# Expert-outer tile order, weights two deep, sorts inside the first expert, and PSUM banks evicted in pairs, in a fused Fourier-mixing and expert kernel

## The chip, the cores and the metric

The kernel runs on one core of a Trainium2 chip. The metric is the time of one execution on the device in microseconds (us); lower is better. An execution varies by about 1% (the unchanged kernel on chip A: 655.30 to 660.46). The runs of this study fell on at least four chips, called A to E here (A's number is not on record, so A may be D or E), and the unchanged kernel doesn't take the same time on all of them: 657.55 us on A, 696.86 on B, 695.48 on C, 659.18 on D, 658.26 on E (medians). So times are compared only with runs of the unchanged kernel in the same rounds on the same chip, and between chips only landmarks inside the traces are compared.

Engines are named as in the profile: PE is TensorE, PEld its weight loads, DVE VectorE, ACT ScalarE, POOL GpSimd, SP SyncE. PSUM is the memory that TensorE writes its results to; a *bank* is a tile of 512 f32 values for each of 128 partitions here. A result is *evicted* when ScalarE or VectorE copies it out, after which its bank is written again (in the first sorts after the change TensorE waits 0.90 to 2.13 us at a time for that). The *granted clock* is the profile's figure for the share of TensorE's full speed that was granted to it (0.50 to 0.98 in the stretches shown before the experiments). A weight is *turned* when TensorE multiplies it by a fixed matrix before its first use.

## The reference, cut to what matters

```python
def _attn_ref(x):                          # x: (8, 2496, 256)
    X = np.fft.fft(np.fft.fft(x, axis=1), axis=2)
    return X.real
def _moe_ref(x, w_gate, w1, w2):           # x: (19968, 256); 8 experts, F = 1024
    cap = N // E
    order = np.argsort(-(x @ w_gate).flatten())
    for idx in order:                      # best score first
        tok, e = idx // E, idx % E
        if assigned[tok] >= 0 or counts[e] >= cap: continue
        assigned[tok] = e; counts[e] += 1
    for e in range(E):
        out[assigned == e] = np.maximum(x[assigned == e] @ w1[e], 0.0) @ w2[e]
```

The kernel does the transform as matrix products. Tokens whose expert the first selection settles are sorted by expert with 0/1 matrices (five "strips" of sorted tokens) and form 40 *early tiles* of up to 384 tokens. The others are settled by further selection rounds, mostly VectorE work, which run while TensorE does early tiles. When the rounds are over, the tokens' places are computed (an "inverse placement"), and 16 *late tiles* are gathered from DRAM by GpSimd. Every 128 output rows go out through one indirect scatter, also issued by GpSimd: 168 scatters and 48 gathers in all.

## The kernel before

A PSUM bank is its own tile here:

```python
    def big_ps(nm):
        return spread_ps("h", 3, [P, 512], FT, nm)      # 3 banks, one more later on
    def transform(n):
        ps = []
        for r in range(2):                              # two halves, two banks
            fps = big_ps("fftps").rearrange("p (b d) -> p b d", b=NB)
            ...                                         # 20 matmuls into fps
            ps.append(fps)
        nc.scalar.copy(ev, ps[0])
        nc.vector.tensor_tensor(st[:, :, 0, :], ev, ps[1], op=AL.add)
        nc.vector.tensor_tensor(st[:, :, 3, :], ev, ps[1], op=AL.subtract)
    def up(d, fcs):                                     # first expert matmul, tile "hps"
        for fc in fcs:
            hps = big_ps("hps")
            ...                                         # 2 matmuls
            take(d["hid"][:, fc, 0:n], hps[:, 0:n], True)   # eviction on ScalarE or VectorE
```

`take` gives an eviction to whichever of ScalarE and VectorE has less to do by an estimate kept while the program is built. `down` makes the second expert matmul (tile `ops`), evicts it to an output buffer `ot` (8 of them), and scatters that. A tile is worked off in three parts ("thirds"); the order of tiles is strip by strip, and the gathers come in threes from tile 28 on:

```python
            for part, (fcs, b0) in enumerate((((0, 1, 2), 0), ((3, 4, 5), P), ((6, 7), 2 * P))):
                for step in aside.get((j, part), ()):
                    step()                              # sorts, weights, gathers
                up(tiles[j], fcs)
                down(tiles[j - 1], b0, group)
                pace()                                  # some of the selection rounds
    tiles = [early_tile(t, e) for t in range(NT) for e in range(E)]
    G0 = 28
    for m, d in enumerate(late):
        j = G0 + (3 * m) // 2 if m < 8 else 40 + m - 8
        at(j, 1, lambda d=d: (place_all(), gather(d)))
```

Of the kernel before, what the change touches and what calls it, by code (L numbers as in the profile page):

```python
# [18 lines left out]
B = 8  # L19
# [34 lines left out]
KC = 64  # L54
SYNC = None
# [11 lines left out]
def kernel(  # L67
# [14 lines left out]
    MAN = {mybir.EngineType.PE, mybir.EngineType.DVE, mybir.EngineType.Activation, mybir.EngineType.Pool}  # L82

# [174 lines left out]
    for b in range(B):  # L258
# [29 lines left out]
        if b % 4 == 3:  # L288
            for n0, nn in ((0, 4), (4, 4), (8, 2)):
                ytp = psl.tile([P, 4, P], FT, tag="tp", bufs=4, name="ytp")  # L290
                for u in range(nn):
                    nc.tensor.transpose(ytp[:, u, :], yt[:, n0 + u, :], identf)
                src = ytp[:, 0:nn, :].rearrange("p n (b f) -> p n b f", f=32)
                for s_ in range(2):
                    dh = yhl[:, n0:n0 + nn, s_, 0, :].rearrange("p n (b e) -> p n b e", e=E)[:, :, b - 3:b + 1, :]
                    dl = yhl[:, n0:n0 + nn, s_, 1, :].rearrange("p n (b e) -> p n b e", e=E)[:, :, b - 3:b + 1, :]
                    sv = src[:, :, :, s_ * E:(s_ + 1) * E]
                    nc.scalar.copy(dh, sv)
                    nc.vector.tensor_tensor(dl, sv, dh, op=AL.subtract)
        for i, r in tab_plan[b + 1]:  # L300
# [6 lines left out]
    lg = asg_c.tile([P, E, GC], FT, name="lg")  # L307
    with tc.tile_pool(name="pslog", bufs=1, space=PS) as pslog:
# [43 lines left out]
    def misc():  # L352
        return psr[0].tile([P, 512], FT, tag="misc", bufs=1, name="misc")
# [7 lines left out]
    def big_ps(nm):  # L361
        return spread_ps("h", 3, [P, 512], FT, nm)
# [21 lines left out]
    mv = asg.tile([P, GC], FT, name="mv")  # L384
    mvv = mv.rearrange("p (b q k) -> p b q k", b=B, q=4)
    nc.gpsimd.memset(mv, -1.0e9)  # L386
    tail0 = asg.tile([P, 1], FT, name="tail0")
    tail1 = asg.tile([P, 1], FT, name="tail1")
    head1 = asg.tile([P, 1], FT, name="head1")
    nc.gpsimd.tensor_scalar(tail0, in0=iota_p, scalar1=113.0, scalar2=2.0e9, op0=AL.is_ge, op1=AL.mult)  # L390
    nc.gpsimd.tensor_scalar(tail1, in0=iota_p, scalar1=112.0, scalar2=2.0e9, op0=AL.is_ge, op1=AL.mult)
    nc.gpsimd.tensor_scalar(head1, in0=is0, scalar1=2.0e9, scalar2=None, op0=AL.mult)
    for q in range(4):
        nc.gpsimd.tensor_scalar(mvv[:, :, q, NK - 1], in0=mvv[:, :, q, NK - 1],
                                scalar1=tail0 if q < 2 else tail1, scalar2=None, op0=AL.add)
        if q % 2 == 1:
            nc.gpsimd.tensor_scalar(mvv[:, :, q, 0], in0=mvv[:, :, q, 0], scalar1=head1, scalar2=None, op0=AL.add)


# [19 lines left out]
    rampw_i = asg.tile([P, EW + 2], I32, name="rampw_i")  # L419
# [5 lines left out]

    def payloads():
        pay_i = rampw_i[:, 0:GC]
        nc.gpsimd.iota(rampw_i, pattern=[[1, EW + 2]], base=1, channel_multiplier=0)
        nc.gpsimd.tensor_copy(rampw, rampw_i)
        for q, (s1, s2) in enumerate(((0, 1), (2, -1), (1, -1), (1, 1))):  # L430
            for par in range(2):
                nc.gpsimd.iota(pay_i.rearrange("p (n k b q) -> p n k b q", n=4, k=NK, b=2)[:, :, :, par, q],
                               pattern=[[2 * S, 4], [s2 * P, NK]], base=PAY0 + S // 2 * s1 + par * S,
                               channel_multiplier=s2)
        nc.vector.tensor_scalar(pay_i, in0=pay_i, scalar1=16, scalar2=None, op0=AL.logical_shift_left)
        nc.vector.tensor_copy(payr, pay_i.bitcast(FT))
        for n in range(4):
            nc.gpsimd.iota(pay_i[:, n * 8 * NK:(n + 1) * 8 * NK].rearrange("p (f k) -> p f k", k=NK),
                           pattern=[[1, 8], [8, NK]], base=n * 8 * NK + 1, channel_multiplier=0)
        nc.vector.tensor_copy(place, pay_i)  # L440
        for n in range(4):
            nc.gpsimd.iota(pay_i[:, n * 8 * NK:(n + 1) * 8 * NK].rearrange("p (f k) -> p f k", k=NK),
                           pattern=[[1, 8], [8 * P, NK]], base=n * 8 * P * NK + PAY0, channel_multiplier=8)
        nc.vector.tensor_scalar(pay_i, in0=pay_i, scalar1=16, scalar2=None, op0=AL.logical_shift_left)
        nc.vector.tensor_copy(payb, pay_i.bitcast(FT))
# [16 lines left out]
    def choose(first):  # L462
# [19 lines left out]
        yield SYNC  # L482
        for e in range(E):
            nc.scalar.activation(cjunk, dd[:, e, :], ACT.Relu, bias=1.0, scale=K_CNT, accum_out=cnt[:, e:e + 1])  # L484
            busy["A"] += 0.33
            if e % 4 == 3:
                yield 0.3
        nc.scalar.copy(cnt_x.rearrange("p (e g) -> p e g", g=NG), cnt[:, :, None].to_broadcast([P, E, NG]))
        yield SYNC
# [3 lines left out]
        chosen["src"] = src  # L493
# [3 lines left out]
    def lowest():  # L497
        nc.vector.scalar_tensor_tensor(wa, in0=dd, scalar=K_LOW, in1=chosen["src"], op0=AL.mult, op1=AL.subtract)
        yield 1.4
        for e in range(E):  # L500
            nc.vector.max(lists[:, e, :], wa[:, e, :])
            nc.scalar.copy(lists_x[:, :, e * NG:(e + 1) * NG], lists[:, e, :, None].to_broadcast([P, 8, NG]))
            busy["A"] += 0.3
            if e % 4 == 3:
                yield 1.0
        yield SYNC
        lt = psr[0].tile([P, 8, P], FT, tag="lt", bufs=1, name="lt")
# [4 lines left out]
        yield SYNC  # L512
# [64 lines left out]
    def raise_first(aside):  # L577
        run(lowest())
        run(search(2))
        aside(found["low"], found["wid"], found["lo0"])  # L580

        def finish():
            yield from search(1)
            yield from settle()
        return finish
# [46 lines left out]
    def inverse(hi1, lo1, pay, w, ncol):  # L632
        ramp8 = ramps[8]
        inv_ps = psr[0].tile([P, 512], FT, tag="lt", bufs=1, name="inv_ps")
        for c0 in range(0, ncol, 8):
            cs = slice(c0, c0 + 8)
            oh = moe.tile([P, 2, P * 8], BF, tag="w1raw", bufs=2, name="oh")
            o_lo = oh[:, 0, :].rearrange("p (a b) -> p a b", b=8)
# [68 lines left out]
    def first_strips(low, wid, lo0):  # L707
# [8 lines left out]
        nc.vector.scalar_tensor_tensor(lev, in0=lev, scalar=moved, in1=fits, op0=AL.min, op1=AL.max)  # L716
        bps = psm.tile([P, 512], FT, tag="o", bufs=1, name="lev_ps")
# [6 lines left out]
                                       op0=AL.is_ge, op1=AL.mult)  # L724
        v = asg.tile([P, GC], FT, tag="sl_v", bufs=1, name="sl_v")
# [22 lines left out]
        nc.vector.scalar_tensor_tensor(spot, in0=v, scalar=1.0, in1=has, op0=AL.add, op1=AL.mult)  # L748
        nc.vector.tensor_scalar(t2, in0=t3, scalar1=3, scalar2=None, op0=AL.arith_shift_right)
# [5 lines left out]
        early["has"] = has  # L755
# [4 lines left out]
    run(choose(True))  # L760
    finish_round = raise_first(first_strips)
    payloads()
# [4 lines left out]
    def choose_rest():  # L767
        yield from choose(False)
        nc.vector.scalar_tensor_tensor(ohb, in0=dd, scalar=0.0, in1=rest[:, None, :].to_broadcast([P, E, GC]),
# [101 lines left out]

    def transform(n):
        b0, kc = NB * (n // NK), n % NK
        ks = slice(kc * P, (kc + 1) * P)
        st = stg.tile([P, NB, 4, D], BF, tag="stage", bufs=3, name="stage")
        ps = []
        for r in range(2):
            fps = big_ps("fftps").rearrange("p (b d) -> p b d", b=NB)
            for d0, d1, tab in ((0, P + 1, hi["c" + "EO"[r]]), (P + 1, D, hi["s" + "EO"[r]])):
                for i in range(NK):  # L880
                    nv = rows_of(i, r)
                    nc.tensor.matmul(fps[:, :, d0:d1], lhsT=tab[:nv, i, ks],  # L882
                                     rhs=zball[:nv, b0:b0 + NB, 2 * i + r, d0:d1],
                                     start=(i == 0), stop=(i == NK - 1))
            ps.append(fps)
        ev = stg.tile([P, NB, D], FT, tag="ev", bufs=2, name="ev")
        nc.scalar.copy(ev, ps[0])
        nc.vector.tensor_tensor(st[:, :, 0, :], ev, ps[1], op=AL.add)  # L888
        nc.vector.tensor_tensor(st[:, :, 3, :], ev, ps[1], op=AL.subtract)
        for q in range(2):  # L890
            nc.scalar.activation(st[:, :, 1 + q, P + 1:D], st[:, :, 3 * q, P + 1:D], ACT.Copy, bias=0.0, scale=-1.0)  # L891
            nc.gpsimd.tensor_copy(st[:, :, 1 + q, 0:P + 1], st[:, :, 3 * q, 0:P + 1])  # L892
        nc.sync.dma_start(td_v[n].rearrange("p f d -> p (f d)"), st.rearrange("p b q d -> p (b q d)"))


    def wtile(nm, tag, bufs):
        return moe.tile([P, 2 * F], BF, tag=tag, bufs=bufs, name=nm)

    w1t = [wtile("w1t%d" % e, "w1t%d" % e, 1).rearrange("p (a f) -> p a f", a=2) for e in range(E)]
    w2t = [wtile("w2t%d" % e, "w2t%d" % e, 1).rearrange("p (a d) -> p a d", a=F // P) for e in range(E)]  # L900
    w1raw = {}

    def load_w(e):
        w1raw[e] = wtile("w1raw", "w1raw", 2).rearrange("p (a f) -> p a f", a=2)
        nc.gpsimd.dma_start(w1raw[e], moe_w1[e].rearrange("(a p) f -> p a f", p=P))
        nc.gpsimd.dma_start(w2t[e], moe_w2[e].rearrange("(a p) d -> p a d", p=P))

    def turn_w(e):
        for j in range(2):
            for fh in range(2):  # L910
                wps = big_ps("wps")
                fs = slice(fh * 512, (fh + 1) * 512)
                for dc in range(2):
                    nc.tensor.matmul(wps, lhsT=mt_b[:, dc, j * P:(j + 1) * P], rhs=w1raw[e][:, dc, fs],
                                     start=(dc == 0), stop=(dc == 1))
                take(w1t[e][:, j, fs], wps)

    for e in range(E):
        load_w(e)
    for n in range(4 * NT):  # L920
        transform(n)
    swap_sb()
    busy["A"] = busy["D"] = 0.0
# [263 lines left out]
```

## Time and profile before

Median 657.55 us over four runs on chip A (655.30 to 660.46); the profiled execution has a span of 658.9 us and a granted TensorE clock of 0.917.

Landmarks of that trace (first and last start of a tile's instructions):

| | us |
|---|---|
| transforms | 151.3 to 219.9 |
| first sort matmul | 235.5 |
| first expert matmul | 249.3 |
| inverse placement | 463.9 to 477.5 |
| gathers from | 478.5 |
| last early / last late expert matmul | 543.1 / 645.5 |

The first view gives busy time by stretches of the span. Columns: from and to in us, the length, then busy us of each engine (with the number of instructions), the granted TensorE clock, the DMA engines' busy share, GB/s.

```profile
151.30:220.00 68.70, 53.23 (x422) 43.56 (x423) 50.98 (x117) 29.01 (x83) 32.81 (x84) 0.90 0.90 215
220.00:249.30 29.30, 16.12 (x130) 8.94 (x128) 13.88 (x41) 11.39 (x25) 6.99 (x9) 0.94 0.86 234
249.30:450.00 200.70, 187.79 (x1507) 137.41 (x1504) 153.91 (x451) 146.37 (x397) 85.82 (x82) 0.97 0.29 91
450.00:478.50 28.50, 7.76 (x82) 6.85 (x81) 25.27 (x83) 2.01 (x6) 2.02 (x3) 0.58 0.04 13
478.50:550.00 71.50, 71.50 (x583) 54.04 (x582) 41.74 (x102) 37.40 (x83) 53.00 (x54) 0.98 0.24 76
550.00:646.00 96.00, 84.97 (x678) 64.50 (x677) 42.69 (x89) 40.30 (x90) 73.15 (x76) 0.96 0.24 75
```

The engines are in the order PE, PEld, DVE, ACT, POOL. Between 450 and 478.5 TensorE nearly stands still (7.8 of 28.5 us) while VectorE works (25.3).

The second view is TensorE's timeline inside the transforms: start, length, engine, line, operation, tiles, shapes, count, and in brackets an idle time before it with what ended it.

```profile
190.87 0.72 PE L882 MATMUL fftps<-zball,hi_cE 128*128 128x258 bf16 x5
191.43 0.71 PE L882 MATMUL fftps<-zball,hi_sE 128*128 128x254 bf16 x5
192.41 0.72 PE L882 MATMUL fftps<-zball,hi_cO 128*128 128x258 bf16 x5 [0.27 <-DVE stage L889]
192.97 0.71 PE L882 MATMUL fftps<-zball,hi_sO 128*128 128x254 bf16 x5
193.52 0.72 PE L882 MATMUL fftps<-zball,hi_cE 128*128 128x258 bf16 x5
```

From the waits of that stretch (what waited, for what, us in total, times, longest):

```profile
PE fftps L882 <- DVE stage L889: 4.5, 3, 2.5
PE misc L491 <- ACT cnt_x L488: 4.4, 1, 4.4
PE fftps L882 <- ACT ev L887: 0.7, 1, 0.7
```

Another view gives the costliest groups: line, engine, operation, shapes, count, busy us and mean ns of one, idle time before it and what ended it. These are the evictions of 384 columns ("+1 forms" are some of 352):

```profile
L860 ACT ACTIVATE hb<-hps 128x384 bf16<-128x384 f32 (+1 forms) x293 | 131.1, 490 | 74.0 <-PE hps L1036 68.5
L864 DVE TENSOR_SCALAR hb<-hps 128x384 bf16<-128x384 f32 (+1 forms) x155 | 82.3, 546 | 50.4 <-PE hps L1036 37.6
```

Another gives the waits between 550 and 620 (what waited, for what, us in total, times, longest). The end is limited by output buffers (`ot`) whose scatter has not landed:

```profile
ACT ot L860 <- DMA out_dram<-ot,rows_l: 34.6, 13, 4.6
DVE ot L866 <- DMA out_dram<-ot,rows_l: 20.3, 6, 4.1
```

### The profile page before, as it was taken

The page shows a single profiled execution, that of the slowest core. Times are in us where ns is not written, and L with a number is a line of the kernel's source. Part 1 is how long each engine was busy: PE and PEld are TensorE (multiplying, and loading weights), DVE is VectorE, ACT ScalarE, POOL GpSimd, SP SyncE. Part 2 cuts the span into 40 slices and gives each one's busy share as a digit, 9 for nine tenths or more (in the row PEclk, how much of TensorE's full clock was granted, in tenths as well). Part 3 has the DMA queues.
Part 4 walks back from the last instruction along what each step waited for, and adds up shares of the span by engine and source line. Part 5 has one row for each costly group of instructions (what it writes and reads, how often), then busy time and mean ns, then how long its engine had stood idle before and what let it go on. Part 6 is the DMA issues. An engine that isn't in the chain of part 4 may idle for free.

```text
span 658.9 us, 11484 instructions
## 1 busy us (share of the span) xinstructions
PE 517.7 (79%) x4003; PEld 359.7 (55%) x4003; DVE 428.8 (65%) x1062; ACT 362.5 (55%) x842; POOL 318.1 (48%) x399
## 2 busy tenths in 40 slices
PE   0675697666688659989979999894399999887894
PEld 0321232265467435657757777673377777665673
DVE  3887694368785457868858878768875555433451
ACT  1478776764145446767767867753055455333451
POOL 8786410006433411534524444433067777777774
PEclk9979867879789998999989999997589999989898
DMA  8778440003996784422222323221012222222221
GB/s 257 220 238 265 145 151 1 0 2 46 239 268 247 233 246 107 118 70 90 98 69 96 116 91 103 88 80 39 0 55 80 82 78 87 72 66 67 78 83 56
DMA packets 35169, 74.63 MB, mean 113 GB/s; under 512 B 6115, under 2 KB 14349, under 8 KB 35104
## 3 DMA queue, kind: packets, MB, share of 16 engines
q0 software_dynamic: 23296, 42.10, 24.5%
q1 hardware_dynamic: 11808, 31.73, 14.1%
q8 instruction: 33, 0.54, 0.4%
q14 instruction: 32, 0.26, 0.1%
HBM read 51.26 MB, written 32.24 MB: 127 GB/s over the span
## 4 chain that ended last, share of the span: by engine, by line
PE 55%; DVE 13%; ACT 12%; DMA 9%; POOL 5%; issue 4%; POOLq 0%; DVEq 0%; ACTq 0%; SPq 0%
PE hps L1036 18%; PE ops L1047 17%; PE yps L284 6%; PE fftps L882 3%; PE sps L960 3%; DMA out_dram<-ot,rows_l 3%; ACT zball L269 3%; ACT cjunk L484 2%; DMA t_dram<-stage 2%; PE tp L281 2%; POOL xg L1012 1%; DMA w1raw<-in_moe_w_dram 1%; ACT tf L244 1%; ACT yt L286 1%; DMA xl<-t_dram 1%
## 5 line engine op out<-in xcount | busy, mean ns | idle before, releaser
L1047 PE MATMUL ops<-w2t,hb 128*128 128x256 bf16 (+1 forms) x1344 | 177.6, 276 | 11.0 <-ACT ot L860 11.0
L1051 POOL DMA_INDIRECT out_dram<-ot,rid x120 | 124.2, 1035 | 121.1 <-ACT ot L860 78.0
L860 ACT ACTIVATE hb<-hps 128x384 bf16<-128x384 f32 (+1 forms) x293 | 131.1, 490 | 74.0 <-PE hps L1036 68.5
L1047 PEld LDWEIGHTS <-hb 128*128 128x128 bf16 (+1 forms) x1344 | 134.2, 100 | 46.3 <-issue 14.2
L1036 PE MATMUL hps<-xs,w1t 128*128 128x384 bf16 x640 | 132.2, 333 | 6.3 <-DVE xs L866 4.0
L1036 PEld LDWEIGHTS <-w1t 128*128 128x128 bf16 x896 | 87.0, 100 | 53.7 <-issue 15.1
L864 DVE TENSOR_SCALAR hb<-hps 128x384 bf16<-128x384 f32 (+1 forms) x155 | 82.3, 546 | 50.4 <-PE hps L1036 37.6
L860 ACT ACTIVATE ot<-ops 128x256 f32<-128x256 f32 x111 | 42.5, 383 | 87.8 <-PE ops L1047 44.0
L284 PE MATMUL yps<-zt,g_sb 128*16 128x512 f32 (+1 forms) x96 | 50.7, 636 | 28.6 <-ACT zt L283 28.4
L1012 POOL DMA_INDIRECT xg<-t_dram,ids_l x48 | 46.4, 966 | 39.5 <-DVE wa L671 25.2
L866 DVE COPY ot<-ops 128x256 f32<-128x256 f32 (+1 forms) x57 | 24.2, 424 | 61.8 <-PE ops L1047 32.0
L113 POOL DMA_INDIRECT xb<-in_x_dram,mir_i x40 | 52.9, 1321 | 20.9 <-issue 14.1
L1051 POOL DMA_INDIRECT out_dram<-ot,rows_l x48 | 47.1, 982 | 16.1 <-issue 7.0
L1036 PE MATMUL hps<-xt,w1t 128*128 128x384 bf16 (+1 forms) x256 | 49.7, 328 | 0.0
L960 PE MATMUL sps<-pt,xl 128*128 128x192 bf16 x320 | 33.5, 248 | 4.3 <-DMA xl<-t_dram 2.7
L281 PEld LDWEIGHTS tp<-identf,z 128*128 128x128 f32 x160 | 20.5, 163 | 28.2 <-issue 22.7
L860 ACT ACTIVATE xs<-sps 128x384 bf16<-128x384 f32 x65 | 28.7, 489 | 11.9 <-PE sps L960 11.8
L892 POOL COPY stage<-stage 128x258 bf16<-128x258 bf16 x40 | 17.3, 443 | 34.5 <-DVE stage L888 30.5
L891 ACT ACTIVATE stage<-stage 128x254 bf16<-128x254 bf16 x40 | 16.5, 415 | 30.0 <-DVE stage L888 27.4
L284 PEld LDWEIGHTS yps<-zt,g_sb 128*16 128x16 f32 x96 | 6.4, 100 | 48.4 <-ACT zt L283 41.3
L386 POOL MEMSET mv<- 128x160 f32 x1 | 0.2, 231 | 67.2 <-PE fftps L882 67.2
L960 PEld LDWEIGHTS <-xl 128*128 128x128 bf16 x320 | 28.0, 99 | 7.0 <-DMA xl<-t_dram 2.9
(326 smaller groups left out, 834.8 us busy)
## 6 DMA issues: line engine op xcount, KB each, us to landing
t_dram<-stage SPq DMA_DIRECT2D x20, 512.0 KB
xl<-t_dram SPq DMA_DIRECT2D x20, 512.0 KB
xa<-in_x_dram SPq DMA_DIRECT2D x8, 1024.0 KB
w1raw<-in_moe_w_dram POOLq DMA_DIRECT2D x8, 512.0 KB, 8.2
w2t<-in_moe_w_dram POOLq DMA_DIRECT2D x8, 512.0 KB, 17.0
out_dram<-ot,rid POOLq DMA_INDIRECT x120, 2.5
xa<-in_x_dram SPq DMA_DIRECT2D x8, 224.0 KB
xg<-t_dram,ids_l POOLq DMA_INDIRECT x48, 2.6
```

What stands on the lines that cost most here:

```text
L113: nc.gpsimd.indirect_dma_start(out=bv[0:n, i, :], out_offset=None, in_=x_pairs, in_offset=bass.IndirectOffsetOnAxis(ap=mir_i[0:n, b * NK + ...
L269: nc.scalar.copy(zball[:, b], z)
L281: nc.tensor.transpose(tp[:, u, :], z[:, n0 + u, blk * P:(blk + 1) * P], identf)
L284: nc.tensor.matmul(yps[pb:pb + 2 * E, 0:nn, :], lhsT=g_sb[:, blk, :], rhs=zt[:, 0:nn, :], start=(blk == 0), stop=(blk == 1))
L860: nc.scalar.activation(dst, src, ACT.Relu if relu else ACT.Copy)
L864: nc.vector.tensor_scalar(dst, in0=src, scalar1=0.0, scalar2=None, op0=AL.max)
L866: nc.vector.tensor_copy(dst, src)
L960: nc.tensor.matmul(sps[:, j2 * EW:(j2 + 1) * EW], lhsT=xl[:, 2 * g + cc, j2 * P:(j2 + 1) * P], rhs=pt[:, 2 * g + cc, 0:EW], start=(cc == 0 ...
L1012: nc.gpsimd.indirect_dma_start(out=xg[0:nr, q, :], out_offset=None, in_=t_dram, in_offset=bass.IndirectOffsetOnAxis(ap=d["ids"](q, nr), ax ...
L1036: nc.tensor.matmul(hps[:, 0:n], lhsT=w1t[d["e"]][:, j2, fc * P:(fc + 1) * P], rhs=d["x"](j2), start=(j2 == 0), stop=(j2 == 1))
L1047: nc.tensor.matmul(ops[0:nr, 0:D], lhsT=d["hid"][:, fc, b0:b0 + nr], rhs=w2t[d["e"]][:, fc, :], start=(fc == 0), stop=(fc == F // P - 1))
L1051: put = nc.gpsimd.indirect_dma_start(out=out, out_offset=bass.IndirectOffsetOnAxis(ap=d["rows"](b0 // P)[0:nr], axis=0), in_=ot[0:nr, :], ...
```

## The change

Its intent: begin with one expert, so that two experts' weights are enough at the start and only one has to be turned before the first tile; keep the sorts inside the first expert's tiles; halve the number of evictions by evicting two banks at once; and pace the selection rounds evenly over the tiles. The parts that matter here (the diff is some 780 lines long, the rest is cut):

```diff
-    def big_ps(nm):
-        return spread_ps("h", 3, [P, 512], FT, nm)
+    def pair_ps(nm):
+        return psm.tile([P, 2, 512], FT, tag="h", bufs=2, name=nm)
 ... transform: both halves in one pair; the combination of transform n is issued within transform n+1
+        pair = pair_ps("fftps")
+        ps = [pair[:, r, :].rearrange("p (b d) -> p b d", b=NB) for r in range(2)]
         for r in range(2):
             ...
+            if r == 0:
+                nc.scalar.copy(ev, ps[0])
 ... up: chunks 2i and 2i+1 share a pair, evicted together
+            k = fc % 2
+            if k == 0:
+                d["hps"] = pair_ps("hps")
             ...
+            if k == 1:
+                take(d["hid"][:, fc - 1:fc + 1, 0:n], d["hps"][:, :, 0:n], True)
 ... sorts (sps) and turned weights (wps) get a pair in the same way
-    tiles = [early_tile(t, e) for t in range(NT) for e in range(E)]
+    tiles = [early_tile(e, t) for e in range(E) for t in range(NT)]
 ... the other strips' sorts stand between the thirds of tiles 0 to 3; weights: 2 and 3 buffers,
     written to DRAM and read back for the late tiles; output buffers 8 -> 12
+            state["credit"] = min(state["credit"] + PACE, PACE)      # PACE = 2.0 us of VectorE per third
+        state["g"] += GRATE                                          # GRATE = 0.75 gathers per third
+        while state["g"] >= 1.0 and state["next"] < len(calls) and state["placed"]:
+            state["g"] -= 1.0
+            ...                                                      # gather_one
```

## The prediction

> **What bounds the kernel now.** The chain of waits is 55% TensorE; busy time by stretches gives four stages. (1) 0 to 151 us, input and logits: untouched. (2) 151 to 249 us, transform, first selection, weights, first sorts: TensorE is busy 69 of 98 us; the timeline shows it waiting on weight loads (4.7 and 1.4 us), a reload (2.7 us) and VectorE, which is busy 65 us. (3) 249 to 478 us, 28 tiles with sorts and selection rounds: TensorE is 94% busy until 450, then works 7 of 28 us, because the rest of the rounds is issued in one block at tile 28. (4) The rest: 5.2 us per tile until 550, then TensorE drops to 0.86 and 0.76 busy. There GpSimd issues an indirect transfer every 1.28 us without a break, and the waits name output buffers not yet written out (35 us on ScalarE, 20 on VectorE, between 560 and 620).
>
> **What the change does.**
> - Stage 2: six of eight weight loads go, transform and selection are interleaved by hand, one expert is turned before tile 0. VectorE's 65 us loses some weight evictions; about 62 remain, so the first expert matmul should come at 217 instead of 249: -32 us.
> - Sorts move into tiles 0 to 3: TensorE about 11.5 us per tile, VectorE 10.3, ScalarE 9.7. Moved, not removed.
> - Paired evictions: a 384-column eviction takes 0.49 us on ScalarE, 256 columns 0.38, so I estimate 0.81 for a pair of 768: 0.17 us saved for each of some 280 pairs. Off TensorE's path; it buys room for the rounds.
> - Rounds spread over tiles 5 to 31: the 20 us block disappears. But 2.0 us of selection per third of a tile exceeds TensorE's 1.75, and the issue order leaves nearly all evictions to ScalarE: I count 138 us on ScalarE, 140 on VectorE, 150 on TensorE for the same 26 tiles. I allow 12% TensorE idle.
> - Gathers: the pacing credit (0.75 per third) also accumulates before placement is ready and is then spent in a loop. The built order shows 36 gathers back to back on GpSimd at tile 31, ahead of tile 30's last output. [...] 36 x 1.28 = 46 us without an output; twelve buffers cover four tiles, 21 us. So about 25 us stall, then 8 us while gathers and outputs share the queue. The old end lost about as much.
> - Added: weights stored and reloaded (16 MB); transfers are only 22 to 30% busy there.
>
> **Sum.** First expert matmul 217; tile 4 at 268; tile 31 at 453; 134 us for the other 25 tiles plus 34 stalled gives 621; end 11 us later: 632 us, range 606 to 652. Chances: faster 0.80, within 2% 0.15, slower 0.05.
>
> **What would show it.** First expert matmul near 217; rounds done by tile 31 without a hole; ScalarE near 90% busy in tiles 5 to 31; one unbroken run of 36 gathers and a TensorE hole of 20 to 30 us around tile 35, waits naming output buffers.
>
> **What would make it wrong.** Rounds on VectorE delaying evictions more than allowed, or the reload queue blocked behind weight stores in the sort stage (slower); a burst absorbed, or faster tiles than three full engines suggest (615 or less).

The sum came to 632 us, range 606 to 652, with 46 us for the 36 gathers. Those 46 us are the estimate, from the order in which the kernel was built and the 1.28 us per transfer in the trace of before. The trace of after shows the 36 gathers in a row from 522.1 to 566.7 us, 44.7 us with no output among them.

## More of the kernel before

The E half of a transform fills one bank, the O half another, and the O half follows with no wait, or a small one for a free bank. Undisturbed, a transform takes TensorE about 2.2 us. All 20 take 68.6 us (151.3 to 219.9), that is 3.4 us each, because of waits for the work around them.

## The result, and the profile after

The change makes the kernel slower: 702.59 us (696.32 to 703.10, four runs) against 657.55, a ratio of 1.066 (95% interval 1.058 to 1.074). A ratio here is the mean time of one kernel's fast runs over that of the other's of the same rounds, so it isn't quite the ratio of the quoted medians. The profiled execution has a span of 700.5 us, granted clock 0.913.

The prediction's sum against what the trace shows, in stages that add up to the span (tile 4 starts about when the last sort is done, so that is the landmark used):

| stage | predicted us | measured us | excess |
|---|---|---|---|
| up to the first expert matmul | 217 | 255.2 | 38.2 |
| from there to the last sort (321.1) | 51 | 65.9 | 14.9 |
| from there to the first gather (522.1) | 185 | 201.0 | 16.0 |
| from there to the end | 179 | 178.4 | -0.6 |
| span | 632 | 700.5 | 68.5 |

Busy time by stretches after the change, cut at the landmarks (columns as before):

```profile
152.10:220.00 67.90, 51.11 (x416) 40.93 (x417) 41.88 (x91) 28.28 (x76) 24.33 (x67) 0.97 0.60 194
220.00:255.20 35.20, 18.41 (x128) 13.46 (x128) 21.99 (x78) 8.36 (x12) 2.49 (x5) 0.59 0.30 105
255.20:326.00 70.80, 51.97 (x520) 39.64 (x519) 37.26 (x156) 37.17 (x51) 11.13 (x11) 0.94 0.49 143
326.00:522.00 196.00, 171.69 (x1270) 122.75 (x1275) 133.08 (x360) 133.45 (x254) 98.32 (x93) 0.97 0.43 111
522.00:606.00 84.00, 54.88 (x399) 38.84 (x399) 20.99 (x29) 22.74 (x38) 63.82 (x67) 0.86 0.33 95
606.00:687.00 81.00, 79.48 (x654) 61.95 (x654) 36.67 (x58) 39.59 (x60) 50.99 (x53) 0.98 0.44 145
```

From 152 to 255 no engine is full: VectorE works 63.9 of 103 us, TensorE 69.5. VectorE's work is what had been predicted (62), but it doesn't set the time. The pause of 450 to 478 is gone, as predicted, and TensorE's idle share from 326 to 522 is 12%, the share that the prediction allowed.

TensorE's timeline in the transforms, after:

```profile
190.71 0.73 PE L911 MATMUL fftps<-zball,hi_cE 128*128 128x258 bf16 x5 [0.99 <-DVE stage L923]
191.28 0.71 PE L911 MATMUL fftps<-zball,hi_sE 128*128 128x254 bf16 x5
192.72 0.72 PE L911 MATMUL fftps<-zball,hi_cO 128*128 128x258 bf16 x5 [0.73 <-ACT ev L915]
193.28 0.71 PE L911 MATMUL fftps<-zball,hi_sO 128*128 128x254 bf16 x5
193.82 0.72 PE L911 MATMUL fftps<-zball,hi_cE 128*128 128x258 bf16 x5
194.39 0.71 PE L911 MATMUL fftps<-zball,hi_sE 128*128 128x254 bf16 x5
195.82 0.72 PE L911 MATMUL fftps<-zball,hi_cO 128*128 128x258 bf16 x5 [0.73 <-ACT ev L915]
```

Each O half now waits for `ev`, ScalarE's copy of the E half (0.73 us each in these lines). The O half doesn't need the copy, it fills the other bank; but the two banks are one tile now, and the trace has TensorE released by that copy in all 20 transforms. An otherwise undisturbed transform takes 3.1 us in place of 2.2. The whole stage is as long as before (67.3 us against 68.6): the new order took the old waits away, as intended, and the pairs put 15.3 us of their own in their place. That the wait comes from the two halves being one tile is shown by experiments 1 and 3 below: with single banks the transforms end at 205.2 us in place of 219.4, with the copy issued after both halves at 205.0. All waits of that kind between 152.1 and 220:

```profile
PE fftps L911 <- ACT ev L915: 15.3, 20, 1.7
```

After the transforms come the sorts of the first strip:

```profile
227.34 1.44 PE L1000 MATMUL sps<-pt,xl 128*128 128x192 bf16 x8 [5.87 <-DVE pt L975]
230.90 1.44 PE L1000 MATMUL sps<-pt,xl 128*128 128x192 bf16 x8 [2.13 <-DVE xs L892]
233.39 1.44 PE L1000 MATMUL sps<-pt,xl 128*128 128x192 bf16 x8 [1.05 <-DVE xs L892]
235.73 1.44 PE L1000 MATMUL sps<-pt,xl 128*128 128x192 bf16 x8 [0.90 <-ACT xs L886]
238.06 1.44 PE L1000 MATMUL sps<-pt,xl 128*128 128x192 bf16 x8 [0.90 <-ACT xs L886]
```

Eight matmuls fill a pair; the next eight always wait until the previous pair has been evicted (`xs`). There should be two pairs in turn. The other one is held by the last transform, whose two additions on VectorE are issued only after these sorts (at 247.0 us in the trace). In the stop and go the granted clock is 0.59 (second line of the stretches): one of these matmuls takes 367 ns (median of the first strip's), against 246 (median of all). Over the 19.4 us of these 64 matmuls it is 0.50. So the low clock goes together with the waits between the sorts: in experiments 14 and 13, where those are mostly gone, the same 64 matmuls take 9.8 and 8.3 us, and from the last transform to the first expert matmul the granted clock is 0.80 and 0.79, in place of 0.59.

In the tiles that have sorts between their thirds (first two lines, 255.2 to 321.1) and in the rounds (last two lines, 321.1 to 522.1), TensorE waits for evictions of `xs` and `w1t` before it gets a bank:

```profile
PE sps L1000 <- ACT xs L886: 4.5, 8, 0.9
PE hps L1136 <- ACT xs L886: 2.7, 6, 0.6
PE wps L952 <- ACT w1t L886: 5.6, 5, 1.1
PE hps L1136 <- ACT w1t L886: 3.9, 5, 0.8
```

The end behaves as predicted: 36 gathers in a row (GpSimd takes 0.94 us for each, with 0.30 us between them, so about 1.25 us), the output buffers run out, TensorE stops for 21.9 us.

```profile
548.23 0.49 PE L1136 MATMUL hps<-xs,w1t 128*128 128x384 bf16 x2
570.66 1.44 PE L1136 MATMUL hps<-xs,w1t 128*128 128x384 bf16 x4 [21.94 <-ACT hb L886]
```

The waits between 522 and 606 name the buffers:

```profile
ACT ot L886 <- DMA out_dram<-ot,rid: 39.8, 7, 24.1
DVE ot L892 <- DMA out_dram<-ot,rid: 14.5, 5, 4.6
```

And this is the saving that the pairs brought, per eviction:

```profile
L886 ACT ACTIVATE hb<-hps 128x768 bf16<-128x768 f32 (+1 forms) x175 | 137.7, 803 | 60.8 <-PE hps L1136 60.3
L890 DVE TENSOR_SCALAR hb<-hps 128x768 bf16<-128x768 f32 (+1 forms) x49 | 45.8, 937 | 40.2 <-PE hps L1136 30.9
```

Two evictions of 384 columns cost 2 x 490 = 980 ns of ScalarE, one of 768 costs 803: 0.18 us saved (the medians of the pure forms, 490 and 810 ns, give 0.17). The prediction's 0.17 was right. On VectorE a saved eviction is worth 2 x 546 - 937 = 155 ns, 0.155 us.

### The profile page after: what moved, and what is told of

Its sections match the earlier page's. It is cut to its first block, busy times and chain, and to the rows that moved or that the text cites. A ratio compares the mean times of both kernels' runs of the same rounds, so it can differ in the third digit from the quotient of the medians.

```text
span 700.5 us, 11216 instructions
## 1 busy us (share of the span) xinstructions
PE 524.2 (75%) x3994; PEld 363.1 (52%) x4003; DVE 392.5 (56%) x949; ACT 365.9 (52%) x651; POOL 324.9 (46%) x399
## 4 chain that ended last, share of the span: by engine, by line
PE 43%; ACT 17%; DVE 15%; POOL 10%; issue 10%; DMA 4%; POOLq 0%; DVEq 0%; ACTq 0%
PE hps L1136 10%; PE ops L1148 10%; PE fftps L911 6%; PE yps L295 5%; POOL out_dram L1152 5%; PE sps L1000 4%; POOL xg L1104 4%; ACT zball L280 3%; PE wps L952 2%; ACT xs L886 2%; ACT w1t L886 2%; DMA out_dram<-ot,rid 2%; ACT cjunk L500 1%; ACT ev L915 1%; DMA xl<-t_dram,ids_l 1%
## 5 line engine op out<-in xcount | busy, mean ns | idle before, releaser
L1152 POOL DMA_INDIRECT out_dram<-ot,rid x120 | 126.8, 1056 | 166.9 <-ACT ot L886 111.4
L886 ACT ACTIVATE hb<-hps 128x768 bf16<-128x768 f32 (+1 forms) x175 | 137.7, 803 | 60.8 <-PE hps L1136 60.3
L1136 PE MATMUL hps<-xs,w1t 128*128 128x384 bf16 x640 | 132.2, 336 | 44.7 <-ACT hb L886 34.7
L892 DVE COPY ot<-ops 128x256 f32<-128x256 f32 (+1 forms) x62 | 26.3, 424 | 125.4 <-PE ops L1148 71.3
L886 ACT ACTIVATE ot<-ops 128x256 f32<-128x256 f32 x106 | 40.6, 383 | 97.0 <-PE ops L1148 46.3
L890 DVE TENSOR_SCALAR hb<-hps 128x768 bf16<-128x768 f32 (+1 forms) x49 | 45.8, 937 | 40.2 <-PE hps L1136 30.9
L1000 PE MATMUL sps<-pt,xl 128*128 128x192 bf16 x320 | 39.1, 282 | 25.1 <-DVE pt L975 10.5
L886 ACT ACTIVATE xs<-sps 128x768 bf16<-128x768 f32 x33 | 26.2, 809 | 47.7 <-PE sps L1000 47.7
L1000 PEld LDWEIGHTS <-xl 128*128 128x128 bf16 x320 | 32.8, 112 | 30.6 <-issue 29.2
L975 DVE TENSOR_SCALAR pt<-rampw,spot 128x193 bf16<-128x193 bf16 x160 | 30.0, 272 | 6.0 <-PE sps L1000 6.0
L1104 POOL DMA_INDIRECT xg<-t_dram,ids_l x30 | 28.3, 945 | 9.2 <-issue 8.8
```

The lines of the kernel that those rows point to most:

```text
L886: nc.scalar.activation(dst, src, ACT.Relu if relu else ACT.Copy)
L890: nc.vector.tensor_scalar(dst, in0=src, scalar1=0.0, scalar2=None, op0=AL.max)
L892: nc.vector.tensor_copy(dst, src)
L975: nc.vector.tensor_scalar(marks[n][:, f, 0:EW + 1], in0=rampw[:, 0:EW + 1], scalar1=spot[:, c:c + 1], scalar2=None, op0=AL.is_equal)
L1000: nc.tensor.matmul(sps[:, g - g0, j2 * EW:(j2 + 1) * EW], lhsT=xl[:, 2 * g + cc, j2 * P:(j2 + 1) * P], rhs=pt[:, 2 * g + cc, 0:EW], start= ...
L1104: nc.gpsimd.indirect_dma_start(out=d["xg"][0:nr, q, :], out_offset=None, in_=t_dram, in_offset=bass.IndirectOffsetOnAxis(ap=d["ids"](q, nr ...
```

## The experiments

Theory A: four PSUM banks handed out as two pairs are only two things that can be given back, and three waits follow: the O half on the copy (transforms), the last transform's held pair (first sorts), and half-filled `hps` pairs that are held over the sorts and the other work between the thirds (tiles 0 to 3, and the rounds). Rivals: B, the hand-made order of the instructions or the weights' transfers; C and D concern the end: the burst of gathers starves the outputs (C), or GpSimd's queue bounds the end whatever the order (D).

### 1. Four single banks (chip B)

```diff
-        return psm.tile([P, 2, 512], FT, tag="h", bufs=2, name=nm)
+        return [psm.tile([P, 512], FT, tag="h", bufs=4, name=nm) for _ in range(2)]
+    ... and fftps, wps, sps, hps written and evicted bank by bank
```

> The changed kernel with every pair of PSUM banks taken apart again into single banks (four of them, one eviction each); all else as changed. Theory A (TensorE waits because two pairs are too few slots and a half-filled or unfinished pair holds both its banks): first expert matmul at about 235 us instead of 255, sorts of tiles 0 to 3 about 10 us shorter than the 71 us, total near 670 us. Theory B (the hand order makes VectorE and ScalarE wait in the wrong sequence; pairs only help): first expert matmul stays within 3 us of 255, and 280 more evictions at 0.17 us make the total 700 us or more.

Measured: transforms end at 205.2 us (after the change: 219.4), first expert matmul 233.4 (255.2), last sort 289.3 (321.1), gathers from 477.1 (522.1). Time 684.12 us against 696.86 (medians); only two of its four runs (682.74, 675.22) count as fast and the other two as slow, so there is no interval. With the order and the transfers untouched, 45 us come back before the gathers. That speaks for A and against B.

### 2. The last transform's additions before the sorts (chip B)

```diff
+    while unit():
+        pass
+    while pending:
+        pending.pop(0)()
     sort_mark(0)
```

> Only the last transform's two VectorE additions are issued before the first sorts instead of after them, so that its pair of banks comes free. Theory A: the eight sorted pairs of tile 0 now alternate between two slots, the stretch from the first sort matmul to the weight turning shrinks from 20 us to about 13, first expert matmul at about 249, total 695. Theory B: nothing moves but the additions, total within 2 us of 702.

Measured: the first sort at 225.4, the first expert matmul at 241.4: 16.0 us between them in place of 27.9 (227.3 to 255.2). Last sort 306.9, gathers from 508.7. Time 720.71, ratio to before 1.036 (1.030 to 1.042). The held pair is one of the causes, worth about 12 us.

### 3. The copy after both halves (chip B)

```diff
-            if r == 0:
+            if r == 1:
                 nc.scalar.copy(ev, ps[0])
```

> Only ScalarE's copy of the first half of a transform is issued after the second half's matmuls instead of between the halves. Theory A: the wait of TensorE on that copy (15.3 us in 20 waits) goes, a transform takes about 2.4 us instead of 3.1, first expert matmul at about 244, total 691. Theory B: VectorE's order is what sets the pace, the transforms then wait on VectorE as long as they did on ScalarE, total within 3 us of 702.

Measured: transforms end at 205.0, first sort 213.9, first expert matmul 242.3, last sort 308.9, gathers from 510.6; 716.84 us, ratio 1.026 (1.020 to 1.033). The copy is issued *later* than before and the stage gets 13 us *shorter* (53.9 us from the first to the last transform matmul, in place of 67.3), and no wait for `ev` is left in it: the wait was made by reading one half of a tile while the other half was still to be written.

### 4. No gathers saved up before the placement (chip B)

```diff
-        state["g"] += GRATE
+        if state["placed"]:
+            state["g"] += GRATE
```

> Only the pacing credit of the gathers starts at zero when placement is ready, so that no 36 gathers stand in a row. Theory C (the run of 36 gathers blocks the outputs): the TensorE hole of about 22 us after tile 31 goes, gathers and outputs share GpSimd until about tile 52, some 12 us of stall remain of 29, total about 683. Rival D (GpSimd's total of 96 transfers sets the end, whatever their order): the stall only moves to later tiles, total within 5 us of 702.

Measured: the gathers are spread (first group 526.1 to 630.2 us), the longest single wait of TensorE's expert matmuls from then on is 6.3 us, but the time is 724.32, ratio 1.038 (1.032 to 1.045). The late tiles take 120 us (590.8 to 710.6) where the change on chip A took 91. Both totals that had been expected (683, and within 5 us of 702) were missed. This edit says nothing yet: chip B is 40 us slower than A with the unchanged kernel too, and the changed kernel had not run on it.

### 5 and 6. Before and after again, on one chip (chip C)

> The unchanged kernel, profiled again, as a reference on this run's chip. On an earlier chip it took 697 us against 658 us on the first one, and no profile showed where. Theory D (only the end depends on the chip: output rows land later, buffers come free later, GpSimd and TensorE wait for each other there): the landmarks up to the start of the gathers stay within 5 us of the first profile (first expert matmul 249, gathers start 478), and anything slower than 660 us lies after that. Rival (the chip is slower in everything, for example a lower granted clock): the landmarks scale by the same per cents from the beginning.

> The changed kernel, unedited, so that it and its variants can be compared on one chip. Theory D: landmarks as in the first profile to the start of the gathers (first expert matmul 255, inverse 501, gathers 522 us); if this chip is the slow one, TensorE stops 10 to 13 us after the gathers start (as in the variants with one part undone) instead of 26 us after, and the time is about 725 us, 1.04 of before. If that early stop was made by the variants' edits and not by the chip, it stops after 26 us here too and ends near 700 us.

Measured for before: 697.44 us (one run); first expert matmul 248.9, gathers from 476.8, both within 2 us of chip A's trace; from the gathers' start to the end 218.8 us in place of 180.4. Measured for after: 731.48 us against 695.48, ratio 1.052 (1.047 to 1.057); first sort 230.1, inverse placement from 503.1, gathers from 524.6, then 205.1 us to the end in place of 178.4; TensorE first stops 12.1 us after the gathers' start, as D had expected for a slow chip, in place of 26.7. So chip C differs from A only from the start of the gathers, in both kernels. Chip B looks the same: in experiment 4, whose edit acts only from there on, the gathers start 371.3 us after the first transform, on chip A 370.0. The loss is made before the gathers on both kinds of chip (43.6 us on A, 47.8 on C); on C 13.7 us of it come back after them.

What differs at the end could be narrowed down, not settled. Pairing the k-th copy into an output buffer with the scatter that had that buffer before (from the timelines of ScalarE, VectorE and GpSimd), the unchanged kernel reuses a buffer as early as 1.2 us after its scatter's instruction ended on GpSimd on chip A (560 to 620), and never sooner than 14.6 us on chip C (500 to 640), where engines wait for it. The same pairing gives 1.5 us for the changed kernel on chip A (522 to 640) and never less than 20.0 us for experiment 2 on chip B (508 to 660). GpSimd's time per gather (966 and 969 ns, medians) and the order are the same, the granted clock nearly (0.917 and 0.907). No run here shows why buffers come free later on chips B and C.

### 7. Pairs kept, the three waits taken away (chip C)

The edits of 2 and 3, and the tile split so that no pair is half filled at the end of a part:

```diff
-            for part, (fcs, b0) in enumerate((((0, 1, 2), 0), ((3, 4, 5), P), ((6, 7), 2 * P))):
+            for part, (fcs, b0) in enumerate((((0, 1, 2, 3), 0), ((4, 5), P), ((6, 7), 2 * P))):
```

> Keeps the pairs, takes away the three waits made by them: last transform's additions before the sorts; the first half's copy after both halves; an expert tile split 4+2+2 so that no pair is left half filled across a sort. Theory A (the pairs' two slots cause the lost time before the gathers): transforms end 205, first expert matmul 232 (228 to 237), sorts end 285 to 295, inverse 462 to 476, as good as or better than four single banks, which gave 233, 289 and 455. Rival B (the hand order or the weights' transfers cause it): first expert matmul stays above 240 and sorts take over 62 us more. Time: 0.97 to 1.01 of before.

Measured: transforms end at 204.4, first expert matmul 230.1, last sort 288.3, inverse placement from 455.8, gathers from 477.3; 688.96 us, ratio to before 0.992 (0.987 to 0.997), where the changed kernel in the same rounds has 1.052. A's landmarks are met (the inverse placement came even 6 us before the range). With the pairs, the transfers, the burst and, apart from these three edits, the order all kept, the whole loss is gone. The three savings nearly add up: 13, 12 and 20 us (experiments 3, 2 and 8) against 47.3 us here. From the gathers' start it takes 206.1 us, as the changed kernel (205.1).

### 8. Only the split (chip D)

> Of the three edits of the last test only the split of an expert tile 4+2+2, so that no pair of PSUM banks is left half filled across a sort. Theory A: nothing changes before the first expert matmul (255 to 258 us as in the change itself); the first four tiles shrink by 5 to 10 us (sorts end 312 to 319 in place of 321 to 324) and the rounds after them by 5 to 12 us, so that the inverse placement starts at 482 to 495 in place of 501 to 503. If the split does nothing and the two earlier edits made all of the gain, the first four tiles keep 66 us and the rounds 179 us.

Measured: first expert matmul 255.5, last sort 313.4, inverse placement from 481.1 (1 us before the range), gathers from 502.5; 682.90 us against 659.18 (one run). Nothing before the first expert matmul, 8 us in the first tiles (57.9 in place of 65.9), 12 us in the rounds (189.1 in place of 201.0). The waits for `xs` and `w1t` shrink (255.5 to 313.4, then 313.4 to 502.5):

```profile
PE sps L1000 <- ACT xs L886: 0.9, 4, 0.2
PE hps L1136 <- ACT xs L886: 1.1, 5, 0.2
PE hps L1136 <- ACT w1t L886: 1.2, 5, 0.2
```

So the half-filled pairs cost most of the 20 us, in the tiles that have sorts between their thirds and in those where weights are turned there. A rival is that another split of the thirds helps by itself. With single banks, which have no pairs to hold, these two stretches take 55.9 and 187.8 us with the old split (experiment 1) and 52.0 and 185.1 with the new one (experiment 13, which has other edits too), so up to 6.6 of the 20 us may be the split's own.

### 9. Single banks and a faster pace of the rounds (chip C)

```diff
-PACE = 2.0
+PACE = 3.0
```

> Four single banks as in the first experiment, and the rounds paced at 3.0 us of VectorE per third of a tile in place of 2.0. Against the first experiment: inverse at 455 becomes about 400 to 415 (the 166 us from the sorts' end shrink as the rounds' share per third grows by half), gathers start about 425 to 435. Theory D (the end is bound by what GpSimd still has to issue, so gathers that start earlier, where GpSimd idles half the time, shorten it): the span falls by 10 us or more below the first experiment's, ratio below 0.97 of before. Theory C (the burst of 36 gathers in a row starves the output buffers whenever it comes): the hole in TensorE moves to about 440 with the same 20 to 50 us, and the ratio stays at 0.98.

Both theories missed. The inverse placement came at 437.4, not at 400 to 415, and the time is 709.67, ratio 1.021 (1.014 to 1.028), worse than experiment 1. The trace says why it is worse: from the gathers' start on, TensorE works 191.9 us, in experiment 1 only 141.6. A third with more of the rounds in it takes longer: between the last sort and the gathers it did the first matmuls of 20.5 tiles in 180.1 us, in experiment 1 of 28.5 in 187.8. Earlier gathers were bought with later matmuls. Why the rounds didn't speed up more was not tried; the `pace` code returns at every point where a result from TensorE is needed, once per third, so it may be the number of thirds and not the pace that counts.

### 10 and 11. The three edits without the burst, at 0.75 and at 1.5 gathers per third (chip D)

> The three edits that take the pairs' waits away, and no gathers saved up before the placement (0.75 gathers per third of a tile from then on, no burst). Landmarks to the gathers as without the second part (inverse 456, gathers 477). Theory C (the burst alone makes TensorE's hole): the stretch from the gathers' start to the end falls from 206 to about 165 us, time 645, 0.93 of before. Theory D (GpSimd's queue and late output buffers bound the end, whatever the order of its work): it falls only to about 197 us as in the change with this edit alone, time 675 to 680, 0.97 to 0.98 of before.

> The same with 1.5 gathers per third of a tile in place of 0.75, still none saved up. Theory D: GpSimd's work is the same, so the stretch from the gathers' start to the end is within 6 us of that at 0.75 (about 195 us, time 670 to 680); TensorE is slow in the first 32 thirds and free of waits in the later ones. Theory C: a rate closer to the burst's loses more, 10 us or more slower than 0.75.

Measured at 0.75: gathers from 478.6, then 167.4 us to the end; 647.95 us against 659.18, ratio 0.981 (0.977 to 0.985). At 1.5: gathers from 472.0, then 166.2 us; 642.66, ratio 0.976 (0.973 to 0.980). On this chip, which is of A's kind, it is as theory C says: without the burst the end falls from 178.6 us (experiment 8, the same chip) to 167. On chip B (experiment 4), where buffers come free late, it had fallen only to 197.6. The rate itself hardly matters, as D had said and C had not. (The 5 us between the two medians are there before the gathers start; in the two profiles the first transform alone comes 3.6 us apart.)

### 12. Eight output buffers in place of twelve, with the burst (chip D)

> The three edits with the burst as in the change, and 8 output buffers in place of 12. If output buffers are what TensorE runs out of in the burst, its hole starts 4 buffers earlier, about 4 thirds of a tile or 8 to 10 us, and the end comes about 10 us later (span 690 to 698). If anything else stops it, for example the weights' reload from DRAM, the span stays at 683.

Measured: gathers from 475.6 and TensorE's hole from 493.6 on (the last matmuls before it started at 492.81), 18 us after the gathers' start in place of 24.7 (experiment 8, the same chip) to 26.7 (chips A and E); 659.46 us (one run), 182.1 us from the gathers' start to the end in place of 178.6. The expected span was for the slower kind of chip; the 10 us by which the end was to come later were only 3.5. TensorE's line at the end of the hole:

```profile
492.81 0.81 PE L1140 MATMUL hps<-xs,w1t 128*128 128x384 bf16 x4
525.08 1.44 PE L1140 MATMUL hps<-xs,w1t 128*128 128x384 bf16 x4 [31.45 <-DVE hb L890]
```

Four buffers fewer, a hole that starts 7 to 9 us sooner and is 31.5 us long in place of 21.9 to 23.9, and waits that name the output buffers (49.8 us on ScalarE and 46.4 on VectorE between 475 and 560): it is output buffers that run out.

### 13, 14 and 15. Pairs or single banks, once the waits are gone (chip E)

Three kernels on one chip: 13 is the mended kernel (edits of 2, 3, 7 and 4, 1.5 gathers per third) with four single banks as in experiment 1, 14 the mended kernel with its pairs, 15 the changed kernel.

> Differs from the next run in one thing: four single PSUM banks evicted one by one in place of two pairs. If pairing gains what the prediction counted (0.17 us of ScalarE or VectorE for each of some 280 pairs, but off TensorE's path), the landmarks to the gathers are the same within 4 us (first expert matmul 228 to 234, inverse 450 to 458) and the times agree within 1%. If evictions were what bounds the rounds, the single banks are 10 us or more slower there (sorts' end to inverse 175 or more in place of 165); if two slots are still too few even so, the single banks are 5 us or more faster.

> The mended kernel of the earlier call again (pairs without their three waits, 1.5 gathers per third, none saved up), on the chip of the other two runs. If this chip is like the first (before near 658): 640 to 646, ratio 0.97 to 0.98. If it is like the two where buffers come free later (before near 696): landmarks to the gathers the same, the end 190 to 200 us after the gathers' start, 665 to 680, ratio 0.955 to 0.98.

> The changed kernel on the same chip, to compare: about 1.05 to 1.07 of before on either kind of chip (700 or 730), with the first expert matmul at 255 to 258 and the inverse at 500 to 503, 45 to 50 us later than the mended kernel. If the mended kernel's gain were the chip's and not the edits', the two differ by less than 20 us here.

| chip E | us (median) | ratio to before (658.26) | first expert matmul | last sort | gathers from |
|---|---|---|---|---|---|
| changed kernel | 698.39 | 1.062 (1.057 to 1.068) | 252.3 | 318.6 | 519.0 |
| mended, pairs | 642.00 | 0.976 (0.971 to 0.981) | 229.3 | 286.2 | 472.9 |
| mended, single banks | 635.60 | 0.967 (0.962 to 0.972) | 227.3 | 279.3 | 464.4 |

The single banks are 6.4 us ahead. The intervals of the ratios just overlap, but these kernels ran in the same rounds: the means of their six runs differ by 6.6 us with a standard error of 1.9. So the pairs gain nothing even with those three waits gone; five of the 8.5 us at the gathers' start come from the first tiles (52.0 us to the last sort, against 56.9). In the first sorts, mended with pairs and then with single banks:

```profile
213.71 2.72 PE L1000 MATMUL sps<-pt,xl 128*128 128x192 bf16 x16 [7.17 <-DVE pt L975]
217.34 4.44 PE L1000 MATMUL sps<-pt,xl 128*128 128x192 bf16 x32 [0.91 <-DVE xs L892]
```

```profile
213.47 2.72 PE L1003 MATMUL sps<-pt,xl 128*128 128x192 bf16 x16 [7.16 <-DVE pt L978]
216.71 5.07 PE L1003 MATMUL sps<-pt,xl 128*128 128x192 bf16 x48 [0.52 <-DVE xs L895]
```

Now sixteen matmuls or more run without a wait, in place of eight. With single banks the 64 matmuls of the first strip take 8.3 us (213.5 to 221.8), with pairs 9.8 (213.7 to 223.5), in the changed kernel 19.4. What is left before the sorts, 7.2 us, is VectorE's: it has to finish the selection first. The stretches from the last transform to the first expert matmul, pairs and then single banks:

```profile
203.90:229.30 25.40, 14.48 (x131) 11.33 (x130) 22.40 (x79) 8.93 (x14) 2.67 (x5) 0.80 0.48 177
```

```profile
203.00:227.30 24.30, 13.18 (x129) 10.22 (x129) 23.57 (x81) 8.45 (x19) 2.67 (x5) 0.79 0.55 202
```

Here, and only here, VectorE is nearly full (22.4 of 25.4 us, with single banks 23.6 of 24.3), as the prediction had assumed for the whole stage.

The mended kernel with single banks is the best version: it beats both the kernel before and the changed one on chip E. It was not run on a chip of the slower kind.

## Why the prediction was wrong

The prediction was 632 us, faster by 4%; the change is 6.6% slower.

- **The step that failed** is the first of the sum: "VectorE's 65 us loses some weight evictions; about 62 remain, so the first expert matmul should come at 217 instead of 249". VectorE's work was sized rightly (63.9 us measured), but the step took an engine's busy time for the length of the stage. It came at 255.2. In its place TensorE's waits for PSUM set the pace: two pairs are two slots. Shown by experiments 3 (13 us, the copy's wait), 2 (about 12 us, the held pair) and 7 (together: 230). The profile of before had hardly any of either wait (0.7 us for `ev`), and the diff showed both edits; asking of each PSUM tile who still reads it when its other half is written would have found them.
- Of the 38 us, about 25 are these two waits. Some 12 remain in the mended kernel too (229.3 against 217): on chip E VectorE works 40.7 of the 54.4 us of the transforms, and is nearly full only after them.
- **The same cause, twice more**: the tiles with the sorts were predicted at 51 us and took 65.9; the rounds' stretch was predicted at 185 and took 201.0. Experiment 8 takes 8 and 12 us from them by the split alone, most of it the held pairs'; mended, the latter takes 186.7. So 185 is about what this stretch takes without the held pairs, though not for the prediction's reasons: mended, TensorE works 171.5 of 185.9 us there (150.1 + 21.4 in the two stretches from 287.0 to 472.9), 8% idle. The prediction had counted less work (150 us for 26 tiles, where the stretch holds the first matmuls of 28.5) and allowed more idle time (12%), and the two errors nearly cancel: that part of the sum is luck.
- **The pairs' gain** was sized rightly per eviction (0.17 predicted, 0.18 measured) and called "off TensorE's path". It also was to buy room for the rounds; ScalarE was predicted near 90% busy there and was 68% (133.5 of 196), so no room was needed. Experiments 13 and 14 show that nothing is lost by giving the saving up.
- **The end** was right: 36 gathers in a row, a hole of 20 to 30 us (21.9, starting 26.6 us after the first gather), waits that name the output buffers, 179 us predicted and 178.4 measured. Experiment 12 confirms the buffers as the cause, 10 and 11 the burst, on chips of this kind.
- **The gain that was expected from the order itself** (4%) is mostly not there, even without the waits. With the burst kept, experiment 7 is at 0.992 of before. On chip E the mended kernels reach 0.967 to 0.976 (635.6 and 642.0 us), near the 632 predicted, but 10 to 12 us of that come from taking the burst away, which the prediction had counted as a loss to bear, and in the faster one 6 us from giving the pairs up. With pairs and burst kept, the mended kernel would be at an estimated 652 to 654 us there (642.0 and these 10 to 12), 1% below before.
- The weights' reload, named as what could go wrong, did not: from 255 to 522 no wait on a transfer is among the waits of the trace, and in experiment 7 the transfers are unchanged.

## What to carry to other kernels

Merging two PSUM banks into one tile halved the number of things that can be given back (four to two), and made one half wait for the reader of the other (15.3 us in 20 waits); before trading banks for fewer evictions, list for every pair who still holds it when the next one is wanted, across any other work that stands in between. Busy time of the fullest engine was no forecast of a stage's length here: from 152 to 255 us it was 69.5 of 103 us; where no engine is full, as there, look for who holds the buffers. A pacing credit that grew while it couldn't be spent came out as a burst here (36 gathers in a row); it cost 10 to 12 us on chips of A's kind, because the output buffers behind it ran out.
